# A chunked DeltaNet recurrence feeding a GELU network on one core: the factor g folded into the block inverse, one transposition replaced by ScalarE copies

## The chip, the core and the metric

The kernel runs on one core of a Trainium2 chip. The core has five engines, each with its own queue of instructions that it works through in order: TensorE (PE, matrix products; PEld is its loading of weights), VectorE (DVE), ScalarE (ACT), GpSimd (POOL) and SyncE (SP, which here only issues DMAs). The metric is the device time of one execution in microseconds (us), the median of several runs. The profile is of one execution, and its times count from that execution's start.

## What is computed

`B, H, S, D = 4, 8, 768, 48`. For each of the 32 pairs of batch and head a 48x48 state is carried over 768 steps; the outputs of all heads, laid side by side, are the input of a two-layer network with exact GELU.

```python
k_n = k / (norm(k) + 1e-6)
for t in range(S):
    y[:, :, t] = einsum('bhd,bhde->bhe', q[:, :, t], state)
    v_old      = einsum('bhde,bhd->bhe', state, k_n[:, :, t])
    state     += b_t * einsum('bhd,bhe->bhde', k_n[:, :, t], v_t - v_old)
x = y.transpose(0, 2, 1, 3).reshape(B * S, H * D)        # 3072 x 384
out = gelu(x @ w_in) @ w_out                              # 384 -> 2048 -> 384
```

The two weight matrices arrive as 64-bit floats and are turned into 32-bit ones on the chip. All arithmetic is in 32 bits.

## The kernel before

**Chunks and groups.** The 768 steps are cut into 12 chunks of 64. A tile holds one chunk of two batches: its 128 partitions are two halves `p` of 64 rows. There are two such tiles per chunk (`a` = 0, 1). Two chunks make a group `g` (six groups), with 32 units `u` (tile and head) for each half.

**The inverse of a group.** Inside a chunk the recurrence becomes a triangular system whose matrix is the Gram matrix of the keys, scaled row by row with `g = -beta/norm^2` (`gms`, made in `factors`, L263), plus the identity. Its inverse is built in 32x32 blocks. `eliminate_steps` (L422) does the diagonal blocks of all units at once on VectorE: `flip` (L432) transposes the blocks into `Nu` (L434) and multiplies by a mask that carries g (L435, made by GpSimd at L429), 30 calls of `eliminate` (L437) run two operations each (L442, L444), `diagonal` (L446) sets ones. `back` (L450) then transposes the result three times on VectorE: into `XM` (L453), into the right half of `Zf` (L457, columns 32 to 63), and into the left half of `Zf` (L457 again, columns 0 to 31). `clear` (L461) zeroes the lower rows of the left half, mostly by GpSimd memsets (L469).

**The joins.** The off-diagonal block is made of two small products per unit. Level 0 multiplies `XM` by the Gram block `G` into PSUM (`psJ`); VectorE multiplies this by g into the lower rows of `XM` (L498 in the first group, L528 in the others). Level 1 multiplies `Zf` by `XM`; ScalarE copies the result into the upper rows of the right half of `Zf` (L502, L532). `join` (L477) serves group 0, `join_run` (L504) the others, where the matmuls of level 0 of the later chunk and of level 1 of the earlier chunk are interleaved.

**The steps of a chunk.** `against_state` (L559) forms the products with the state (`psK`, L575), copies `y` (L582, ScalarE), subtracts V (L583, VectorE) and multiplies by g (L584, VectorE) to get W. In chunk 0, where the state is zero, GpSimd multiplies V by `ng` (L565; `ng` is made at L885). `solve` (L591) multiplies by `Zf` (`psU`, L600) and copies to U (L606, ScalarE). `use` and `update` form the output and the new state (L618, L627; `next_state` L632), `read` and `turn` bring x into `xT` (L639 or L641, L662, L663).

**The network.** `fc1` (L684) with the GELU on ScalarE (L686) fills G; `fc2` (L697, chunks 0 and 1) or seven half-size products (L722, later chunks) follow.

**The weights.** `begin`, `exponents`, `mantissas`, `signed` (L214 to L239) decode one of 16 parts: five VectorE operations (L218, L228, L230, L235, L236) with one ScalarE operation (L223) between L218 and L235. `fetch` (L199) loads the next part into the place that has come free.

**What sets the order.** Up to L916 all engines' orders are as written. Behind that a list of steps with due times, in chunks of the network (`plan`, L938), is sorted and issued; VectorE keeps this order, the other engines' orders are set by the scheduler that builds the program. Each engine then follows its own fixed order, and waits by semaphore. PSUM pool `dn` has two buffers and serves `psJ`, `psG`, `psK`, `psU` and `psY` in turn; `psH` and `psO` share two others.

Of the kernel before, what the change touches and what calls it, by code (L numbers as in the profile page):

```python
# [11 lines left out]
ALU = mybir.AluOpType  # L12
# [4 lines left out]
def kernel(  # L17
# [28 lines left out]
    nc = tc.nc  # L46
    B, H, S, D = q.shape
    DM, DF = moe_w_in.shape
    C = 64
# [371 lines left out]

    def eliminate_steps(g):  # L422
        steps = []

        def scales():
            gt = wk.tile([128, HB], F32, tag="gt", name="gt", bufs=1)
            gl = XMs[g] = wk.tile([128, NU, HB], F32, tag="XM", name="XM", bufs=1)
            nc.vector.transpose(gt, gms[g].rearrange("q t h -> q (t h)"))
            nc.gpsimd.tensor_tensor(gl, low, gt.unsqueeze(2).to_broadcast([128, HB, HB]),  # L429
                                    op=ALU.mult)  # L430

        def flip():  # L432
            Nus[g] = wk.tile([128, HB, HB], F32, tag="Nu", name="Nu", bufs=1)
            nc.vector.transpose(Nus[g], Ds[g].rearrange("q u n -> q n u"))  # L434
            nc.vector.tensor_tensor(Nus[g], Nus[g], XMs[g], op=ALU.mult)  # L435

        def eliminate(j):  # L437
            nu = Nus[g]
            n = HB - 1 - j
            tmp = wk.tile([128, HB * HB // 4], F32, tag="tmp", name="tmp")  # L440
            tmp = tmp[:, 0:n * j].rearrange("q (i c) -> q i c", i=n)
            nc.vector.tensor_tensor(tmp, nu[:, j + 1:, j:j + 1].to_broadcast([128, n, j]),  # L442
                                    nu[:, j:j + 1, 0:j].to_broadcast([128, n, j]), op=ALU.mult)
            nc.vector.tensor_tensor(nu[:, j + 1:, 0:j], nu[:, j + 1:, 0:j], tmp, op=ALU.add)  # L444

        def diagonal():  # L446
            flat = Nus[g].rearrange("q i c -> q (i c)")
            nc.vector.memset(flat[:, 0:HB * HB:HB + 1], 1.0)

        def back(x):  # L450
            nu = Nus[g]
            if x == 0:
                nc.vector.transpose(XMs[g].rearrange("q u c -> q c u"),  # L453
                                    nu.rearrange("q i c -> q c i"))
            else:
                cols = slice(HB, C) if x == 1 else slice(0, HB)
                nc.vector.transpose(Zf[g % 2][:, :, cols].rearrange("q u i -> q i u"), nu)  # L457
            if x == 2 and g > 0:
                clear(g)

        def clear(g):  # L461
                for cc in range(2):
                    for p in range(2):
                        part = Zf[g % 2][p * C + HB:(p + 1) * C,
                                         cc * NU // 2:(cc + 1) * NU // 2, 0:HB]
                        if g == cc == p == 0:
                            nc.scalar.mul(part, low[0:HB, 0:HB // 2], 0.0)
                        else:
                            nc.gpsimd.memset(part, 0.0)  # L469

        steps = [(0.3, scales), (3.0, flip)]
        steps += [(0.7, eliminate, j) for j in range(1, HB - 1)]
        steps += [(0.1, diagonal)]
        steps += [(1.9, back, x) for x in range(3)]
        return steps + [(0.0, clear, 0)] if g == 0 else steps

    def join(g, ts, level, copy=nc.scalar.copy):  # L477

        xm, zf, off = XMs[g], Zf[g % 2], Gs[g]
        gm = gms[g].rearrange("q t h -> q (t h)")  # L480
        psJ = dn("psJ").rearrange("q b (u n) -> q b u n", n=HB)
        for i, u in enumerate(range(ts[0] * H, (ts[-1] + 1) * H)):
            for p in range(2):
                top = slice(p * C, p * C + HB)
                low_ = slice(p * C + HB, (p + 1) * C)
                rows, to = (top, low_) if level == 0 else (low_, top)
                nc.tensor.matmul(psJ[to, i // (2 * H), i % (2 * H), :],
                                 lhsT=(xm if level else off)[rows, u, :],
                                 rhs=zf[rows, u, HB:C] if level else xm[rows, u, :],
                                 start=True, stop=True)  # L490
        for i in range(0, len(ts), 2):
            us = slice(ts[i] * H, (ts[min(i + 1, len(ts) - 1)] + 1) * H)
            n = us.stop - us.start
            for p in range(2):
                top = slice(p * C, p * C + HB)
                low_ = slice(p * C + HB, (p + 1) * C)
                if level == 0:
                    nc.vector.tensor_tensor(  # L498
                        xm[low_, us, :], psJ[low_, i // 2, 0:n],
                        gm[low_, us].unsqueeze(2).to_broadcast([HB, n, HB]), op=ALU.mult)  # L500
                else:
                    copy(zf[top, us, HB:C], psJ[top, i // 2, 0:n])  # L502

    def join_run(g, ts0, ts1):  # L504

        xm, zf, off = XMs[g], Zf[g % 2], Gs[g]
        gm = gms[g].rearrange("q t h -> q (t h)")
        sets = []
        for level, ts in enumerate((ts0, ts1)):
            if ts:  # L510
                psJ = dn("psJ")[:, 0].rearrange("q (u n) -> q u n", n=HB)
                sets.append((level, slice(ts[0] * H, (ts[-1] + 1) * H), psJ))
        for i in range(2 * H):
            for p in range(2):
                for level, us, psJ in sets:
                    u = us.start + i
                    top = slice(p * C, p * C + HB)
                    low_ = slice(p * C + HB, (p + 1) * C)
                    rows, to = (top, low_) if level == 0 else (low_, top)
                    nc.tensor.matmul(psJ[to, i, :], lhsT=(xm if level else off)[rows, u, :],  # L520
                                     rhs=zf[rows, u, HB:C] if level else xm[rows, u, :],
                                     start=True, stop=True)
        for level, us, psJ in sets:
            for p in range(2):
                top = slice(p * C, p * C + HB)
                low_ = slice(p * C + HB, (p + 1) * C)
                if level == 0:
                    nc.vector.tensor_tensor(  # L528
                        xm[low_, us, :], psJ[low_],
                        gm[low_, us].unsqueeze(2).to_broadcast([HB, 2 * H, HB]), op=ALU.mult)  # L530
                else:
                    nc.scalar.copy(zf[top, us, HB:C], psJ[top])  # L532

# [25 lines left out]
    def against_state(us):  # L559
# [17 lines left out]
        for u in us:  # L577
            if u.c == 0:
                continue
            gm = gms[u.c // 2][:, u.t]  # L580
            u.y = wk.tile([128, H, D], F32, tag="y", name="y")
            nc.scalar.copy(heads(u.y), u.psK[:, 1])  # L582
            nc.vector.tensor_tensor(heads(u.W), u.psK[:, 0], heads(u.V), op=ALU.subtract)  # L583
            nc.vector.tensor_tensor(u.W, u.W, gm.unsqueeze(2).to_broadcast([128, H, D]),  # L584
                                    op=ALU.mult)

    def quarters(ap):

# [261 lines left out]
    signs(0, 2)  # L850
    diagonals(first[3])
    root(n0)
    scales_, flip_, *rows, back0, back1, back2, clear_ = [s_[1:] for s_ in eliminate_steps(0)]
    factors(gms[0], beta_m[:, 0:2].rearrange("q c a h -> q (c a) h"), n0)
    scales_[0]()
    flip_[0]()
    ng = wk.tile([128, NA, H], F32, tag="ng", name="ng", bufs=1)
    for u in first:
        grams([u])
    signs(2, NC)  # L860
# [21 lines left out]
    grams(fourth)  # L882
    for fn, *args in rows:
        fn(*args)
    nc.vector.scalar_tensor_tensor(ng, gms[0][:, 0:NA], -1.0, ns[0], ALU.mult, ALU.mult)  # L885
    back0[0](*back0[1:])
    against_state(first[:NA])
    for u in first:
# [1 line left out]
    back1[0](*back1[1:])  # L890
    for a in range(NA):
        join(0, (a,), 0)
    back2[0](*back2[1:])
    for a in range(NA):
        join(0, (a,), 1)
    clear_[0](*clear_[1:])
    for u in first[NA:]:
        scale_v(u)
    begin(0)
# [27 lines left out]
    def late():  # L927
# [3 lines left out]
        for a in range(NA):  # L931
# [3 lines left out]
            for c in range(5, NC, 2):  # L935
# [4 lines left out]
    plan += [at(0.98, 0.985, [(1.0, load, 3)]),  # L940
             at(1.02, 1.1, [(1.0, join, 0, range(NA, 2 * NA), level) for level in range(2)]),
]
    sums = [(1.0, sum_of_squares, tiles[c, a], h) for c in (2, 3) for a in range(NA) for h in range(H)]
    plan += [at(1.08, 1.5, sums), at(1.51, 1.511, [(1.0, prep, c) for c in (2, 3)]), at(1.65, 1.655, [(1.0, finish_both)]), at(2.97, 2.971, [(1.0, finish, 4)]), at(2.725, 2.726, [(1.0, queries, third)]),
             at(1.12, 1.6, state_steps(1)),
             at(1.75, 2.45, eliminate_steps(1)),
             at(2.64, 2.77, join_steps(1)), at(2.76, 2.985, state_steps(2)),
             at(2.72, 2.721, [(1.0, prep, 4)]), at(2.8, 2.9, [(1.0, grams, [tiles[4, a] for a in range(NA)])])]
    plan += [at(0.995, 1.0, [(1.0, load_v, 2)]), at(2.98, 2.981, [(1.0, sums_of_w)]), at(3.1, 3.11, [(1.0, last_sum_of_w)])]
# [17 lines left out]
    for w in range(3, NC):  # L967
# [6 lines left out]
        if w % 2:  # L974
            plan += [at(w + 0.09, w + 0.092, gram + query), at(w + 0.25, w + 0.95, state_steps(w))]
            if two_ahead:
# [46 lines left out]
```

## Time and profile before

Median of three runs: 669.02 us (667.24, 669.02, 669.72). The profiled execution has a span of 667.6 us.

| engine | busy us | share of the span |
|---|---|---|
| PE | 643.4 | 96% |
| PEld | 563.6 | 84% |
| DVE | 451.9 | 68% |
| ACT | 228.5 | 34% |
| POOL | 82.3 | 12% |

Busy time by stage, from the view of windows (us from the start; DVE is VectorE):

| stage | PE | DVE | ACT | POOL | granted PE clock |
|---|---|---|---|---|---|
| 0 to 20 | 13.40 | 14.50 | 7.16 | 7.04 | 1.00 |
| 20 to 40 | 15.55 | 18.28 | 10.79 | 0.44 | 0.99 |
| 40 to 60 | 15.59 | 18.79 | 13.73 | 10.31 | 0.50 |
| 60 to 80 | 17.49 | 19.53 | 15.26 | 6.18 | 1.00 |
| 80 to 100 | 19.68 | 19.07 | 9.64 | 0.00 | 1.00 |
| 100 to 120 | 19.78 | 19.38 | 11.65 | 1.92 | 1.00 |
| 120 to 160 | 38.84 | 33.07 | 13.90 | 4.97 | 0.96 |
| 160 to 200 | 39.51 | 30.87 | 17.45 | 6.43 | 1.00 |
| 250 to 300 | 50.00 | 31.87 | 15.35 | 7.05 | 1.00 |

The durations that the operations of the change have in this profile, per instruction:

| operation | tile | mean us | count |
|---|---|---|---|
| L453, L457 transposition | 128x1024 | 2.07, 1.92 | 6, 12 |
| L435 VectorE multiply | 128x1024 | 1.23 | 6 |
| L528 VectorE multiply by g | 32x512 | 0.69 | 20 |
| L498 VectorE multiply by g | 32x256, 32x512 | 0.42, 0.69 | 4, 2 |
| L584 VectorE multiply by g | 128x384 | 0.56 | 22 |
| L469 GpSimd memset | 32x512 | 0.54 | 23 |
| L502 ScalarE copy from PSUM | 32x256, 32x512 | 0.36, 0.57 | 4, 2 |
| L532 ScalarE copy from PSUM | 32x512 | 0.57 | 20 |
| L385 ScalarE copy, SBUF to SBUF | 32x512 | 0.62 | 20 |

A busy share says little here: the stages have different limits. The chain of waits, followed back from the last instruction, tells which engine's work ended last at each point, and the timeline of one engine shows what it waited for (in brackets behind a row: how long it sat idle and which instruction released it). Matmul ends are modelled, and one 32-bit matmul has two records.

### The profile page before, as it was taken

The page shows a single profiled execution, that of the slowest core. Times are in us where ns is not written, and L with a number is a line of the kernel's source. Part 1 is how long each engine was busy: PE and PEld are TensorE (multiplying, and loading weights), DVE is VectorE, ACT ScalarE, POOL GpSimd, SP SyncE. Part 2 cuts the span into 40 slices and gives each one's busy share as a digit, 9 for nine tenths or more (in the row PEclk, how much of TensorE's full clock was granted, in tenths as well). Part 3 has the DMA queues.
Part 4 walks back from the last instruction along what each step waited for, and adds up shares of the span by engine and source line. Part 5 has one row for each costly group of instructions (what it writes and reads, how often), then busy time and mean ns, then how long its engine had stood idle before and what let it go on. Part 6 is the DMA issues. An engine that isn't in the chain of part 4 may idle for free.

```text
span 667.6 us, 21705 instructions
## 1 busy us (share of the span) xinstructions
PE 643.4 (96%) x9542; PEld 563.6 (84%) x9542; DVE 451.9 (68%) x921; ACT 228.5 (34%) x605; POOL 82.3 (12%) x82
## 2 busy tenths in 40 slices
PE   6877999999999999999999999999999999999997
PEld 5666776767789989989989989989989989989997
DVE  6999999994799845489846489846479844324022
ACT  3367755704432242242143142143142132122220
POOL 4050300103110021111021111021111010000000
PEclk9966999998999999999999999999999999999999
DMA  9885655303432232511332511211301210100101
GB/s 132 175 253 173 121 170 133 48 1 71 83 45 39 51 52 43 85 32 26 57 53 45 82 27 31 51 19 32 67 3 26 56 18 3 25 2 2 24 1 25
DMA packets 158431, 39.76 MB, mean 60 GB/s; under 512 B 150016, under 2 KB 153216, under 8 KB 158336
## 3 DMA queue, kind: packets, MB, share of 16 engines
q1 hardware_dynamic: 152464, 33.40, 26.5%
q10 hardware_dynamic: 5872, 4.97, 3.3%
q8 instruction: 75, 1.23, 0.8%
q14 instruction: 20, 0.16, 0.1%
HBM read 33.62 MB, written 4.72 MB: 57 GB/s over the span
## 4 chain that ended last, share of the span: by engine, by line
PE 86%; DVE 7%; ACT 3%; issue 2%; DMA 1%; SPq 0%; DVEq 0%
PE psH L684 36%; PE psX L722 12%; PE psY L722 12%; PE psO L697 5%; PE psZ L722 4%; PE psK L575 3%; PE psJ L520 3%; PE psG L367 3%; PE psU L600 2%; PE psY L618 2%; DVE Nu L444 2%; DVE tmp L442 2%; PE psY L627 1%; ACT U L606 1%; PE psX L662 1%
## 5 line engine op out<-in xcount | busy, mean ns | idle before, releaser
L684 PE MATMUL psH<-xT,w_in_sb 128*128 128x256 f32 x1152 | 261.4, 383 | 2.4 <-ACT G L686 2.3
L684 PEld LDWEIGHTS psH<-xT,w_in_sb 128*128 128x128 f32 x1152 | 215.7, 190 | 33.7 <-ACT G L686 3.5
L686 ACT ACTIVATE G<-psH 128x256 f32<-128x256 f32 x192 | 73.3, 382 | 181.8 <-PE psH L684 169.8
L444 DVE TENSOR_TENSOR Nu<-Nu,tmp 128x30 f32<-128x30 f32 (+9 forms) x180 | 62.9, 349 | 6.2
L442 DVE TENSOR_TENSOR tmp<-Nu 128x30 f32<-128x30 f32 (+9 forms) x180 | 60.5, 336 | 5.1
L722 PE MATMUL psX<-w_out_sb,G 128*128 128x192 f32 x320 | 56.2, 329 | 0.0
L722 PE MATMUL psY<-w_out_sb,G 128*128 128x192 f32 x304 | 54.1, 329 | 0.6
L722 PEld LDWEIGHTS psX<-w_out_sb,G 128*128 128x128 f32 x320 | 52.2, 190 | 0.7
L722 PEld LDWEIGHTS psY<-w_out_sb,G 128*128 128x128 f32 x304 | 49.1, 190 | 2.1 <-DVE u L768 1.8
L663 ACT COPY xT<-psX 128x384 f32<-128x384 f32 x24 | 11.4, 478 | 105.0 <-PE psX L662 105.0
L697 PE MATMUL psO<-w_out_sb,G 128*128 128x384 f32 x128 | 45.0, 498 | 0.0
L306 POOL TENSOR_TENSOR n<-n,half 128x16 f32<-128x16 f32 x10 | 29.4, 2937 | 88.2 <-DVE n L281 67.4
L402 DVE TENSOR_TENSOR P<-psG,mask 128x1024 f32<-128x1024 f32 x10 | 12.2, 1224 | 37.0 <-PE psG L367 37.0
L606 ACT COPY U<-psU 64x192 f32<-64x192 f32 x96 | 30.0, 313 | 21.0 <-PE psU L600 19.7
L697 PEld LDWEIGHTS psO<-w_out_sb,G 128*128 128x128 f32 x128 | 23.7, 191 | 14.4 <-DVE w_out_sb L236 0.6
L583 DVE TENSOR_TENSOR W<-psK,V 128x384 f32<-128x384 f32 x22 | 12.1, 552 | 28.8 <-ACT y L582 28.8
L469 POOL MEMSET Zf<- 32x512 f32 x23 | 12.4, 540 | 154.5 <-DVE Zf L457 153.6
L731 DVE TENSOR_TENSOR S<-G 128x512 f32<-128x512 f32 x20 | 13.7, 687 | 25.8 <-ACT G L686 25.7
L332 POOL TENSOR_TENSOR V<-V,n 128x384 f32<-128x384 f32 x18 | 17.3, 968 | 104.5 <-DMA V<-in_v_dram 69.2
L641 DVE TENSOR_TENSOR x<-psY,y 64x192 f32<-64x192 f32 x80 | 28.3, 354 | 0.9
L722 PE MATMUL psY<-T,G 128*128 128x192 f32 x160 | 28.2, 329 | 0.0
L722 PE MATMUL psX<-T,G 128*128 128x192 f32 x160 | 28.1, 329 | 0.0
(138 smaller groups left out, 871.4 us busy)
## 6 DMA issues: line engine op xcount, KB each, us to landing
Kp<-in_k_dram SPq DMA_DIRECT2D x76, 96.0 KB, 3.3
w_out_sb<-in_moe_w_in_dram SPq DMA_DIRECT2D x24, 256.0 KB, 4.3
V<-in_v_dram SPq DMA_DIRECT2D x48, 96.0 KB, 3.1
out_dram<-o_sb ACTq DMA_DIRECT2D x46, 96.0 KB, 2.2
w_raw<-in_moe_w_out_dram SPq DMA_DIRECT2D x10, 384.0 KB, 4.7
Zf<-in_moe_w_out_dram SPq DMA_DIRECT2D x6, 384.0 KB, 3.9
Qp<-in_q_dram SPq DMA_DIRECT2D x64, 32.0 KB, 2.1
Qp<-in_q_dram SPq DMA_DIRECT2D x16, 96.0 KB, 4.2
```

What stands on the lines that cost most here:

```text
L306: nc.gpsimd.tensor_tensor(flat, flat, half, op=ALU.pow)
L367: nc.tensor.matmul(psG[HALF[p], r, i * NP + j, :], lhsT=u.Kt[rows, p, j, :], rhs=(u.Qt if x else u.Kt)[rows, p, j, :], start=True, stop=True)
L442: nc.vector.tensor_tensor(tmp, nu[:, j + 1:, j:j + 1].to_broadcast([128, n, j]), nu[:, j:j + 1, 0:j].to_broadcast([128, n, j]), op=ALU.mult)
L444: nc.vector.tensor_tensor(nu[:, j + 1:, 0:j], nu[:, j + 1:, 0:j], tmp, op=ALU.add)
L520: nc.tensor.matmul(psJ[to, i, :], lhsT=(xm if level else off)[rows, u, :], rhs=zf[rows, u, HB:C] if level else xm[rows, u, :], start=True, ...
L575: nc.tensor.matmul(u.psK[to, x, r, j, :], lhsT=(u.Qt if x else u.Kt)[rows, p, j, :], rhs=St[rows, u.a, p, j, :], start=True, stop=True)
L606: copy(pairs(u.U[HALF[p]], s), u.psU[HALF[p ^ s], p])
L641: nc.vector.tensor_tensor(dst, src, pairs(u.y[HALF[p ^ s]], s), op=ALU.add)
L684: nc.tensor.matmul(psH, lhsT=w_in_sb[:, f // 2, m, f % 2 * 128:(f % 2 + 1) * 128], rhs=xTs[c][:, m, :], start=(m == 0), stop=(m == NM - 1))
L686: nc.scalar.activation(G[:, f, :], psH, ACT.Gelu)
L697: nc.tensor.matmul(u.psO, lhsT=G[:, f, u.a * 128:(u.a + 1) * 128], rhs=w_out_sb[:, f, :], start=(f == 0), stop=(f == NF - 1))
L722: nc.tensor.matmul(ps_, lhsT=lhs[:, f, :], rhs=rhs[:, f, :], start=first and f == 0, stop=f == FH - 1, skip_group_check=not first)
```

## The change

Once the inverse of the diagonal blocks is complete, its columns are multiplied by g (`weigh`, one VectorE operation of 128x1024 per group, between `diagonal` and the transpositions). The later products with g then fall away: the level-0 results are only copied (now by ScalarE), and W is only the difference. The third transposition of `back` is gone; in its place ScalarE copies the upper diagonal blocks from the right half of `Zf` to the left, in four copies of 32x512 per group (`top`: two for the earlier chunk's units, two for the later's), before level 1 overwrites the source. The zeros of the left half are written once per buffer of `Zf` (`clear`, two GpSimd memsets of 32x1024 each), not in every group. `ng` no longer needs g.

```diff
+        def weigh():
+            nc.vector.tensor_tensor(Nus[g], Nus[g],
+                                    gts[0].unsqueeze(1).to_broadcast([128, HB, HB]), op=ALU.mult)
         def back(x):
...
-                cols = slice(HB, C) if x == 1 else slice(0, HB)
-                nc.vector.transpose(Zf[g % 2][:, :, cols].rearrange("q u i -> q i u"), nu)
-            if x == 2 and g > 0:
-                clear(g)
+                nc.vector.transpose(Zf[g % 2][:, :, HB:C].rearrange("q u i -> q i u"), nu)
...
-        steps += [(1.9, back, x) for x in range(3)]
+        steps += [(0.1, diagonal), (1.2, weigh)]
+        steps += [(1.9, back, x) for x in range(2)]
+    def top(g, p, us):
+        part = Zf[g % 2][p * C:p * C + HB, us]
+        nc.scalar.copy(part[:, :, 0:HB], part[:, :, HB:C])
+    def clear(z):
+        for p in range(2):
+            nc.gpsimd.memset(z[p * C + HB:(p + 1) * C, :, 0:HB], 0.0)
...
-                    nc.vector.tensor_tensor(
-                        xm[low_, us, :], psJ[low_, i // 2, 0:n],
-                        gm[low_, us].unsqueeze(2).to_broadcast([HB, n, HB]), op=ALU.mult)
+                    copy(xm[low_, us, :], psJ[low_, i // 2, 0:n])
...
             nc.vector.tensor_tensor(heads(u.W), u.psK[:, 0], heads(u.V), op=ALU.subtract)
-            nc.vector.tensor_tensor(u.W, u.W, gm.unsqueeze(2).to_broadcast([128, H, D]),
-                                    op=ALU.mult)
...
     scales_[0]()
     flip_[0]()
+    clear(Zf[0])
...
-    nc.vector.scalar_tensor_tensor(ng, gms[0][:, 0:NA], -1.0, ns[0], ALU.mult, ALU.mult)
+    nc.vector.tensor_scalar_mul(ng, ns[0], -1.0)
...
     for a in range(NA):
         join(0, (a,), 0)
-    back2[0](*back2[1:])
+    for p in range(2):
+        top(0, p, EARLIER)
     for a in range(NA):
         join(0, (a,), 1)
-    clear_[0](*clear_[1:])
+    for p in range(2):
+        top(0, p, LATER)
...
+    plan += [at(1.7, 1.71, [(1.0, clear, Zf[1])]), at(0.98, 0.985, [(1.0, load, 3)]),
...
+             at(2.47, 2.6, top_steps(1, EARLIER) + top_steps(1, LATER)),
...
-                         at(w + 0.4, w + 1.06, rows[14:-3]), at(w + 1.07, w + 1.2, rows[-3:])]
+                         at(w + 0.4, w + 1.06, rows[14:-2]), at(w + 1.07, w + 1.16, rows[-2:]),
+                         at(w + 1.17, w + 1.29, top_steps(w // 2 + 1, EARLIER)),
+                         at(w + 1.305, w + 1.355, top_steps(w // 2 + 1, LATER))]
```

The level-0 copies of `join_run` (the other groups) are changed in the same way as those of `join`. In the changed program as built, TensorE's order stays as it was but for three places of the second layer of chunk 0 (where two matmuls change sides with a transposition or a join), and ScalarE's queue takes in the copies. For group 1 it holds, one behind the other: the last eight GELUs of chunk 1's first layer, four `top` copies, two squares of k (L278), two level-0 copies of the earlier chunk, two of the later one, then the level-1 copies. In the later groups three `top` copies stand in front of the sixth GELU of the chunk then under way, and one behind it.

More of the change, by code (lines that the diff above doesn't have):

```diff
@@ L423, in eliminate_steps @@
         steps = []
+        gts = []
         def scales():
             gt = wk.tile([128, HB], F32, tag="gt", name="gt", bufs=1)
+            gts.append(gt)
             gl = XMs[g] = wk.tile([128, NU, HB], F32, tag="XM", name="XM", bufs=1)
@@ L455, in back, with top_steps @@
             else:
-                cols = slice(HB, C) if x == 1 else slice(0, HB)
-                nc.vector.transpose(Zf[g % 2][:, :, cols].rearrange("q u i -> q i u"), nu)
-            if x == 2 and g > 0:
-                clear(g)
[L461 to L469, printed above, removed]
+                nc.vector.transpose(Zf[g % 2][:, :, HB:C].rearrange("q u i -> q i u"), nu)
         steps = [(0.3, scales), (3.0, flip)]
         steps += [(0.7, eliminate, j) for j in range(1, HB - 1)]
-        steps += [(0.1, diagonal)]
-        steps += [(1.9, back, x) for x in range(3)]
-        return steps + [(0.0, clear, 0)] if g == 0 else steps
+        steps += [(0.1, diagonal), (1.2, weigh)]
+        steps += [(1.9, back, x) for x in range(2)]
+        return steps
+    def top(g, p, us):
+        part = Zf[g % 2][p * C:p * C + HB, us]
+        nc.scalar.copy(part[:, :, 0:HB], part[:, :, HB:C])
+    EARLIER, LATER = slice(0, NA * H), slice(NA * H, NU)
+    def top_steps(g, us):
+        return [(1.0, top, g, p, us) for p in range(2)]
+    def clear(z):
+        for p in range(2):
+            nc.gpsimd.memset(z[p * C + HB:(p + 1) * C, :, 0:HB], 0.0)
     def join(g, ts, level, copy=nc.scalar.copy):
         xm, zf, off = XMs[g], Zf[g % 2], Gs[g]
-        gm = gms[g].rearrange("q t h -> q (t h)")
         psJ = dn("psJ").rearrange("q b (u n) -> q b u n", n=HB)
@@ L506, in join_run @@
         xm, zf, off = XMs[g], Zf[g % 2], Gs[g]
-        gm = gms[g].rearrange("q t h -> q (t h)")
         sets = []
@@ L527, in join_run @@
                 if level == 0:
-                    nc.vector.tensor_tensor(
-                        xm[low_, us, :], psJ[low_],
-                        gm[low_, us].unsqueeze(2).to_broadcast([HB, 2 * H, HB]), op=ALU.mult)
+                    nc.scalar.copy(xm[low_, us, :], psJ[low_])
                 else:
@@ L579, in against_state @@
                 continue
-            gm = gms[u.c // 2][:, u.t]
             u.y = wk.tile([128, H, D], F32, tag="y", name="y")
@@ L852 @@
     root(n0)
-    scales_, flip_, *rows, back0, back1, back2, clear_ = [s_[1:] for s_ in eliminate_steps(0)]
+    scales_, flip_, *rows, back0, back1 = [s_[1:] for s_ in eliminate_steps(0)]
     factors(gms[0], beta_m[:, 0:2].rearrange("q c a h -> q (c a) h"), n0)
@@ L939 @@
     plan += [at(0.985, 1.26, decode_steps(3, n_in)), at(1.26, 1.65, decode_steps(n_in, NW)), at(1.66, 1.67, [(1.0, late)])]
-    plan += [at(0.98, 0.985, [(1.0, load, 3)]),
+    plan += [at(1.7, 1.71, [(1.0, clear, Zf[1])]), at(0.98, 0.985, [(1.0, load, 3)]),
              at(1.02, 1.1, [(1.0, join, 0, range(NA, 2 * NA), level) for level in range(2)]),
```

## The prediction

> **What bounds the kernel now.** I read the engine shares first, then the chain of waits, then the timelines around the only places where TensorE stands still. TensorE is busy for 643.4 of 667.6 us. From 200 us on it is idle for about 0.1 us in 50, so nothing that VectorE or GpSimd saves there can shorten the run. Its idle time lies before 72 us and at one later place, which the chain of waits shows:
>
> ```profile
> 145.72 2.14 PE psJ L520 x128
> 147.87 1.49 PE psO L697 x4
> 149.35 1.17 issue
> 150.52 1.20 PE psJ L520 x63
> ```
>
> Columns: start, us, what. These are group 1's joins: both chunks' level 0, two matmuls of the second layer, 1.17 us of nothing, then the earlier chunk's level 1. VectorE's timeline (start, us, engine, line, operation) tells why:
>
> ```profile
> 143.32 2.11 DVE L453 STREAM_TRANSPOSE XM<-Nu 128x1024 f32<-128x1024 f32 x1
> 145.32 3.68 DVE L457 STREAM_TRANSPOSE Zf<-Nu 128x1024 f32<-128x1024 f32 x2
> 149.03 2.82 DVE L528 TENSOR_TENSOR XM<-psJ,gm 32x512 f32<-32x512 f32 x4
> ```
>
> Level 1 needs the first two L528, which end at 149.03+1.41 = 150.44; TensorE starts at 150.52. VectorE has been busy since 88 us (decoding, then row steps) with one gap of 0.2 us, so **VectorE's own sequence sets the moment at which TensorE's unbroken stretch to the end can begin**. The gap costs twice. The windows of half a microsecond (window, length, PE, PEld, DVE, ACT, POOL, granted clock, DMA) show the clock halved after it:
>
> ```profile
> 151.50:152.00 0.50, 0.50 (x14) 0.41 (x9) 0.47 (x2) 0.00 (x0) 0.00 (x0) 1.00 0.00 0
> 152.50:153.00 0.50, 0.50 (x2) 0.32 (x1) 0.39 (x1) 0.50 (x2) 0.00 (x0) 0.50 0.00 0
> 155.00:155.50 0.50, 0.50 (x32) 0.50 (x28) 0.00 (x0) 0.09 (x1) 0.50 (x1) 0.50 0.22 24
> 156.00:156.50 0.50, 0.50 (x44) 0.50 (x38) 0.50 (x1) 0.00 (x0) 0.00 (x0) 1.00 0.60 96
> ```
>
> One more wait decides how much VectorE can gain ahead of this. It is the only one of VectorE's between 60 and 119 us:
>
> ```profile
> 83.64 2.58 ACT L606 COPY U<-psU 64x192 f32<-64x192 f32 x8 [0.72 <-PE psU L600]
> 86.25 0.66 ACT L686 ACTIVATE G<-psH 128x256 f32<-128x256 f32 x2
> 86.80 0.94 ACT L223 ACTIVATE w_e<-w_e,lim 128x768 uint32<-128x768 uint32 x1
> ...
> 87.76 0.96 DVE L235 SCALAR_TENSOR_TENSOR w_e<-Zf,w_e 128x768 uint32<-128x768 uint32 x1 [0.58 <-ACT w_e L223]
> ```
>
> The decode waits for L223, which stands in ScalarE's queue behind the copies of U, which wait for TensorE.
>
> [...] half clock from about 152.2 to 155.7[...]. [...] L228 takes 0.97 and 1.19 us beside GpSimd at 47 to 51 us, 0.55 elsewhere.
>
> **The change, part by part.**
>
> *Start, to 59 us.* After the row steps (39.4) VectorE gets `weigh`. No such row exists; the same size with a full second input is L435, 1.23; between 1.15 and 1.3 (a repeated input could read cheaper or not). So `XM` is ready at 42.85 instead of 41.57 and `Zf`'s right half at 44.8 instead of 43.4. GpSimd's W and P (L565, L405) move by the same 1.3 and are not late: P was done at 46.1 and is read at 51. VectorE drops four L498 (1.75) and the second L457 (1.93), so it reaches the decode at 44.7 instead of 47.0. ScalarE's queue grows. From TensorE's first level-0 half (44.1): two copies of 0.36, wait for the second half (45.2), two more to 46.0, two `top` at L385's 0.62 to 47.2, four level-1 copies (L502, 1.45) to 48.7, two `top` to 49.95, L223 to 50.9, then U. Before, U began at 50.59: +0.3. From there to 59 us the chain runs U, L223, x, xT, L223 on ScalarE, so VectorE's 2.3 us end as waiting, whatever GpSimd's products beside the decode (44.7 to 49.6) cost it. The first set of GpSimd memsets moves to about 16 us, where GpSimd had nothing until 39 us.
>
> *59 to 88 us.* VectorE drops two L498 (1.41) and two L584 (1.06): it would be 2.47-0.3, about 2.1 us ahead. ScalarE takes two copies of 0.57 between GELUs; counting its queue from 62.8 us (L223 0.83, squares 0.23, GELU 0.27, as they follow each other in the trace) the GELU that TensorE waits for at 72.25 comes within 0.5 us of before, rather earlier. TensorE's `psU` then ends 0 to 0.5 earlier than its 83.6, and U, one GELU (two before) and L223 let L235 start at about 87.0 instead of 87.76. VectorE waits there for over a microsecond: **of 2.1 us, 0.8 remain**, 0.3 to 1.3.
>
> *88 to 143 us.* Same instructions. The second `clear` (two memsets of about 1 us at some 112 us) lies beside decode operations of L228's kind: 0 to 1 us, I take 0.4. The row steps end 0.4 us earlier than 143.2.
>
> *Group 1's joins.* VectorE: 143.32-0.4 = 142.9, `weigh` to 144.15, `XM` to 146.2, right half to 148.15. ScalarE: four `top` 2.47, two L278 as they follow each other 0.95, two level-0 copies 1.15, waits 0.15 together: 4.7 us behind the transposition, in a queue that had been idle for 14 us before. Level 1 starts at **152.85 instead of 150.52: +2.3**. TensorE, there by 149.3, can't step over it. What is queued behind: the rest of the second layer, `psG`, the later level 1. From level 1's start to the end of the later level 1 the old trace has 150.52 to 157.0, 6.5 us, of which 3.4 at half clock: 4.8 at full clock, and one second-layer matmul (0.65) is now behind: 5.45. With the half clock until 155.7, 1.4 is done by then and 4.05 is left: 159.75, +2.7. If [...] half speed lasts to 159.1: 161.5, +4.4. [...] I take the middle, **+3.5**.
>
> *Groups 2 to 5.* VectorE loses 2.76 (L528), 2.2 (L584), 1.92 and gains 1.23 for each, all beside a full TensorE: 0. Three `top` copies now precede a GELU. In the old trace TensorE needs this GELU's buffer at 236.7 in group 2; VectorE reaches its end of transposition at about 233.9 (L779 at 225.4, row steps 0.4, `weigh`, four short transpositions 2.5, two long ones 3.9), three copies to 235.75, GELU done by 236.15. Slack 0.5: 0, up to 1 us a group. The level-0 copies (0.57 for 0.69, ending about 238.6) are needed at 239.5: 0. The memsets that fall away waited on nobody's path (0.3 us once). DMAs are neither added nor moved; SP's queue is passed by nothing.
>
> Sum on the profile's span: 667.6+3.5 = 671.1. The runs' median is 1.4 above that span, so **672.5**, 0.52% slower. A measurement of this kernel can tell about 0.5%, 3.3 us, from no change.
>
> **The rivals.**
> 1. *Not slower: VectorE keeps its 2.1 us.* If `psU` comes over a microsecond earlier (ScalarE's queue at 62 to 72 us would have to speed up that much), the wait at L235 vanishes. Level 1 then starts at 151.1, the old half-clock window is the only one, and the later level 1 ends at 158.2: +1.2, 670.2. It decides from a lead of some 1.5 us. For it: VectorE's 2.5 us are real. Against: 2.6 us of U copies stand before L223 in both programs.
> 2. *Worse: the `top` copies hold GELUs in groups 2 to 5.* If VectorE is over 0.5 us later there than I count (GpSimd's V products have stretched row steps from 0.41 to 0.99), TensorE stands still for 0.5 to 1 us in each of four groups on top of the 3.5: 676. For it: no other slack is so small. Against: memsets and four L528 have left.
> 3. *Faster.* U starts earlier than before (copies at 0.4 rather than 0.62)[...]: level 1 at 150.3, no window lost: some 665.5. Against: 152.85 would have to fall by 2.5 us.
>
> **How the numbers follow.** Forecast 0.57 (from 671.7 with one half-clock window to 673.4 with two, about half on each side of 672.4), rival 1 0.26, rival 2 0.12, rival 3 0.05. Faster by over 0.5%: 0.05. Within: 0.26 and 0.24 of the forecast, 0.50. Slower: 0.33 and 0.12, 0.45. The forecast's own range is 671.2 to 674; leaving out rival 3 and the upper part of rival 2, the range is 669.0 to 676.0.
>
> **What would show it.** Right: idle of about 3.5 us on TensorE before group 1's first level 1, released by a ScalarE copy into `XM`; four `top` copies directly behind VectorE's transposition; a halved clock for 3.4 to 7 us behind it; a wait of a microsecond or more at L235's counterpart near 87 us; U near 50.9. Wrong: level 1 before 151 us, VectorE without a wait near 87 us, or idle TensorE of over 0.5 us near each later join.

## The result and the profile after

The changed kernel takes 674.78 us (median of four runs, 674.23 to 676.54); the kernel before, run beside it, 668.47 us. The ratio is **1.0102, 95% interval 1.0083 to 1.0122**: 1% slower. The profiled executions have spans of 672.9 and 667.6 us, a difference of 5.3 us. All that follows is accounted on spans. The other microsecond of the medians is not in it: every execution takes 1.7 to 1.9 us more than its span, so the changed kernel's profile is of a typical execution, but the old kernel's is of one that was 0.9 us slower than its median.

The chain of waits at group 1's joins (start, us, what), where the old kernel had 1.17 us of nothing:

```profile
148.59 0.05 ACT Zf L474
...
150.50 0.61 ACT Zf L474
151.12 0.03 issue
151.14 0.94 ACT ksq L278 x2
152.10 0.58 ACT XM L533
152.69 0.59 ACT XM L533
153.28 0.04 issue
153.32 1.42 PE psJ L525 x64
154.74 3.51 PE psO L697 x6
158.25 1.09 PE psG L367 x64
159.34 1.13 PE psJ L525 x64
```

TensorE stands still for 3.28 us until 153.32, and every step in front of it is on ScalarE: four `top` copies (L474), two squares (L278), the first two level-0 copies (L533). VectorE's timeline ahead of that, in the same columns as before:

```profile
143.42 1.23 DVE L454 TENSOR_TENSOR Nu<-Nu,gt 128x1024 f32<-128x1024 f32 x1
144.68 2.06 DVE L460 STREAM_TRANSPOSE XM<-Nu 128x1024 f32<-128x1024 f32 x1
146.65 1.92 DVE L463 STREAM_TRANSPOSE Zf<-Nu 128x1024 f32<-128x1024 f32 x1
148.42 0.94 DVE L281 TENSOR_REDUCE n<-ksq 128x8 f32<-128x384 f32 x2
```

The new multiplication (L454) costs 1.23 us, as the operation of its size did before; VectorE is through at 148.57, 0.5 us before the first L528 began in the old kernel, and then has only a reduction to do. The windows of half a microsecond show the clock (the last three figures are granted clock, DMA share, GB/s):

```profile
152.50:153.00 0.50, 0.00 (x0) 0.00 (x0) 0.00 (x0) 0.49 (x2) 0.00 (x0) 1.00 0.00 0
154.50:155.00 0.50, 0.50 (x11) 0.44 (x7) 0.00 (x0) 0.16 (x1) 0.00 (x0) 0.50 0.93 181
156.50:157.00 0.50, 0.50 (x2) 0.24 (x1) 0.00 (x0) 0.00 (x0) 0.00 (x0) 0.50 0.00 0
157.50:158.00 0.50, 0.50 (x3) 0.14 (x1) 0.00 (x0) 0.00 (x0) 0.00 (x0) 1.00 0.06 6
```

Half clock from about 154.1 to 157.5 (by windows of a quarter of a microsecond): 3.4 us of it again, begun later. The later level 1 ends at 160.48 instead of 157.00: **+3.5 us**.

The rest is at a second place, 380 us later. ScalarE's timeline, then TensorE's, at group 5's joins (in brackets the idle time before, and who ended it):

```profile
537.12 0.38 ACT L686 ACTIVATE G<-psH 128x256 f32<-128x256 f32 x1 [0.91 <-PE psH L684]
538.99 1.90 ACT L474 COPY Zf<-Zf 32x512 f32<-32x512 f32 x3 [1.49 <-DVE Zf L463]
540.80 0.37 ACT L686 ACTIVATE G<-psH 128x256 f32<-128x256 f32 x1
```

```profile
531.74 7.93 PE L684 MATMUL psH<-xT,w_in_sb 128*128 128x256 f32 x36
541.22 1.56 PE L684 MATMUL psH<-xT,w_in_sb 128*128 128x256 f32 x6 [1.54 <-ACT G L686]
```

A GELU stands behind three `top` copies, which wait for VectorE's transposition; TensorE waits 1.54 us for the GELU. In the old kernel these are 42 unbroken matmul records:

```profile
528.26 9.23 PE L684 MATMUL psH<-xT,w_in_sb 128*128 128x256 f32 x42
```

**The account.** Behind the start TensorE has hardly any other idle time (0.1 us in 50), so the distance between two landmarks on it measures what a stretch lost. I use the starts of level 0 in groups 1, 2 and 5 (from TensorE's timeline), in us:

| kernel | span | level 0, group 1 | to group 2 | group 2 to 5 |
|---|---|---|---|---|
| before | 667.6 | 145.65 | 88.75 | 303.01 |
| changed | 672.9 | 146.99 | 90.89 | 304.83 |
| ... with group 1's top copies on VectorE | 674.1 | 146.81 | 92.19 | 304.96 |
| ... with group 5's top copies on VectorE | 671.3 | 146.84 | 91.29 | 303.02 |
| fold alone | 670.8 | 147.25 | 90.39 | 303.01 |
| third transposition alone | 673.0 | 146.02 | 87.84 | 308.64 |
| changed, group 1's level-0 copies on VectorE | 667.5 | 146.54 | 85.94 | 304.80 |
| the same, and group 5's top copies on VectorE | 666.7 | 147.57 | 85.94 | 303.02 |
| third alone, top copies of groups 2 to 5 on VectorE | 664.0 | 144.86 | 85.94 | 303.01 |

Where nothing waits the middle stretch is 85.94 and the last 303.01; the old kernel, too, lost 2.8 us in the middle one, and the changed one 5.0 there and 1.8 in the last. In both, the loss in the middle is the idle time, 1.17 and 3.28 us, and about 1.7 us more, half of the 3.4 us at half clock. The difference between the two is 2.1 + 1.8 us, and 1.3 us by which level 0 of group 1 starts later; the later level 1, which waits for the copies in any case, is 3.5 us later for the first and the third together. The first column contains the start, which differs by up to a microsecond between executions of one program: the copies of U begin at 50.67 to 51.69 in seven programs that are alike up to there. What makes this difference is not shown.

### The profile page after: what moved, and what is told of

Read it like the earlier page. It is cut to its first block, busy times and chain, and to the rows that moved or that the text cites. A ratio compares the mean times of both kernels' runs of the same rounds, so it can differ in the third digit from the quotient of the medians.

```text
span 672.9 us, 21675 instructions
## 1 busy us (share of the span) xinstructions
PE 643.0 (96%) x9542; PEld 562.7 (84%) x9542; DVE 419.9 (62%) x873; ACT 256.4 (38%) x654; POOL 75.8 (11%) x63
## 3 DMA queue, kind: packets, MB, share of 16 engines
q8 instruction: 75, 1.23, 0.8%
## 4 chain that ended last, share of the span: by engine, by line
PE 77%; DVE 14%; ACT 5%; issue 2%; DMA 1%; POOL 1%; SPq 0%; DVEq 0%; ACTq 0%; POOLq 0%
PE psH L684 32%; PE psX L722 12%; PE psY L722 12%; PE psZ L722 4%; PE psK L578 3%; DVE Nu L446 3%; DVE tmp L444 3%; PE psJ L525 3%; PE psG L367 3%; PE psU L600 2%; PE psO L697 2%; PE psY L618 2%; DVE w_e L235 1%; PE psY L627 1%; DVE w_out_sb L236 1%
## 5 line engine op out<-in xcount | busy, mean ns | idle before, releaser
L722 PE MATMUL psZ<-T,S 128*128 128x192 f32 x160 | 27.6, 326 | 0.0
```

Source lines behind the costliest of these rows:

```text
L722: nc.tensor.matmul(ps_, lhsT=lhs[:, f, :], rhs=rhs[:, f, :], start=first and f == 0, stop=f == FH - 1, skip_group_check=not first)
```

## The experiments

Each run is timed against the kernel before on the same chip; ratios are to it. The first four share one theory A: ScalarE's top copies in front of other work are the delay at both places. Against it stands B, VectorE's longer chain, in the first three, and C, that top copies cost wherever they stand, in the fourth.

**1. Group 1's top copies on VectorE.**

```diff
     def top(g, p, us):
-        nc.scalar.copy(part[:, :, 0:HB], part[:, :, HB:C])
+        copy = nc.vector.tensor_copy if g in (1,) else nc.scalar.copy
+        copy(part[:, :, 0:HB], part[:, :, HB:C])
```

> Group 1's four top copies go from ScalarE to VectorE, which has nothing else then; all else as in the changed kernel. Theory A (ScalarE's queue: 2.5 us of top copies and 0.95 us of squares stand between the transposition at 148.57 and the level-0 copies): the first two level-0 copies run at about 148.3 to 149.4, both level 0 and the second layer's products fill TensorE to 150.6, level 1 starts at 150.6 instead of 153.3, the later level 1 ends at about 156 without a half clock, 157.6 with one (160.48 in the changed kernel): 3 to 4.5 us off the span, 668.4 to 670. Theory B (VectorE's chain is what got too long: weigh's 1.2 us and the lost lead): level 1 still after 152 us, at most 1 us off the span, about 672.

674.98 us, ratio 1.0108 (1.0094 to 1.0122), span 674.1: not better than the changed kernel. Theory A as stated falls, and B's forecast, level 1 after 152 us, came true. But VectorE's and then ScalarE's timeline show another cause than the length of VectorE's chain:

```profile
148.42 1.71 DVE L475 COPY Zf<-Zf 32x512 f32<-32x512 f32 x4
150.14 1.01 DVE L281 TENSOR_REDUCE n<-ksq 128x8 f32<-128x384 f32 x2
```

```profile
150.72 0.98 ACT L278 ACTIVATE ksq<-Kp 128x384 f32<-128x384 f32 x2 [11.16 <-DVE n L281]
151.73 2.35 ACT L534 COPY XM<-psJ 32x512 f32<-32x512 f32 x4
```

ScalarE now waits 11 us with nothing to do. The squares of a later chunk's keys (L278) stand ahead of the level-0 copies in its queue, and they wait until VectorE's reduction (L281) has emptied one of their two buffers; VectorE comes to that behind its top copies. In the changed kernel the reduction ran beside ScalarE's top copies, so this wait could not be seen. Level 1 starts at 152.95, and the later one ends at 161.60, for here the clock is at half for 6.8 us (153.0 to 159.8).

**2. Group 5's top copies on VectorE** (the same edit with `g in (5,)`).

> Only group 5's four top copies go from ScalarE to VectorE. Theory A: the GELU that TensorE waits for at 541.2 no longer stands behind three copies, TensorE's 1.54 us of idle time and the 0.28 us after it vanish: 1.8 us off the span, about 671.1, and nothing changes at group 1 (level 1 at 153.3). Theory B (VectorE is late there, with its weigh and the transpositions of Q in front): level 0 is held by XM or by the second transposition in place of the GELU, under 0.5 us off the span, about 672.7.

673.38 us, ratio 1.0083 (1.0069 to 1.0097), span 671.3. The wait at group 5 is gone (303.02), group 1 is nearly as in the changed kernel (level 1 at 153.13, but 1.92 us long in place of 1.42, as in experiment 1, where it runs at half clock; the middle stretch is 0.4 longer). A holds here, and group 5's price of 1.8 us is shown; the two ratios' intervals overlap, so it rests on the trace.

**3. The fold alone.**

The diff is to the changed kernel; the memsets come back with the third transposition.

```diff
-        steps += [(1.9, back, x) for x in range(2)]
+        steps += [(1.9, back, x) for x in range(3)]
...
-    for p in range(2):
-        top(0, p, EARLIER)
+    back2[0](*back2[1:])
...
-             at(2.47, 2.6, top_steps(1, EARLIER) + top_steps(1, LATER)),
```

> The g folding alone: VectorE's third transposition and the memsets of each group are back, no top copies on any engine. TensorE's order is that of the changed kernel. Theory A: level 1 of group 1 at about 150.6, the later level 1 ends at 156 to 157.6, no idle TensorE at group 5, U of chunk 0 about 0.5 us earlier (some 50.6): span 666 to 668, so about as before or up to 0.3% faster than it. Theory B (weigh's 1.2 us on VectorE's chain is the cause, a third transposition in front of nothing changes little): as slow as the changed kernel within 1 us, 672.

672.64 us, ratio 1.0071 (1.0059 to 1.0084), span 670.8: neither theory's number. Group 5 has no wait, as A said. At group 1 the squares wait once more for the reduction, this time behind the third transposition, and level 1 starts at 153.12. ScalarE's timeline:

```profile
150.90 0.97 ACT L278 ACTIVATE ksq<-Kp 128x384 f32<-128x384 f32 x2 [10.90 <-DVE n L281]
```

So no top copy is needed for the delay; it is enough that the level-0 copies have moved to ScalarE, behind the squares.

**4. The third transposition alone** (from the kernel before: `back` with two transpositions, `top`, `top_steps` and `clear` as in the change; no `weigh`).

> The other half alone, built from the kernel before: the third transposition becomes four top copies on ScalarE per group, zeros written once; no weigh, VectorE still multiplies the level-0 results and W by g. TensorE's order is that of the kernel before. Theory A: the level-0 products with g run on VectorE right behind the second transposition (147.3), beside the top copies, so level 1 starts at about 149.4, where TensorE arrives, instead of 150.5; the later level 1 ends 1 to 2.4 us earlier than before's 157.0; at group 5 the GELU is held by about 0.4 us: span 665.5 to 667.5, not slower than before. Theory C (the top copies are the costly part wherever they stand): slower than before by 2 us or more, 670 and above.

674.40 us, ratio 1.0095 (1.0080 to 1.0111), span 673.0: far from A's 665.5 to 667.5, and by the number what C said. Yet group 1 behaved as A said: VectorE does the level-0 products itself at 147.65, level 1 starts at 149.72 where TensorE arrives, no half clock (1.00 granted from 148 to 155), the later one ends at 154.56 (157.00 before). But all of groups 2 to 5 lost. TensorE's timeline has three of the waits:

```profile
232.36 1.56 PE L686 MATMUL psH<-xT,w_in_sb 128*128 128x256 f32 x6 [1.63 <-ACT G L688]
335.05 1.56 PE L686 MATMUL psH<-xT,w_in_sb 128*128 128x256 f32 x6 [1.41 <-ACT G L688]
437.73 1.56 PE L686 MATMUL psH<-xT,w_in_sb 128*128 128x256 f32 x6 [1.41 <-ACT G L688]
```

and ScalarE's timeline shows how, at the second:

```profile
331.08 0.39 ACT L688 ACTIVATE G<-psH 128x256 f32<-128x256 f32 x1 [0.91 <-PE psH L686]
333.35 1.24 ACT L467 COPY Zf<-Zf 32x512 f32<-32x512 f32 x2 [1.88 <-DVE Zf L456]
334.61 0.38 ACT L688 ACTIVATE G<-psH 128x256 f32<-128x256 f32 x1
```

Here the scheduler has put the top copies ahead of the *fifth* GELU of the chunk. In the changed kernel they stand ahead of the sixth in groups 2 to 4, and ahead of the fifth in group 5 alone. GELUs follow each other at 1.29 us, so one place in the queue is worth about the wait. No experiment moved the copies by one place; that the place matters is read from groups 2 to 4 of the changed kernel, where the same copies stand one GELU later and TensorE waits for nothing.

Out of these four came a theory A2: **what delays group 1 is whatever stands in front of the level-0 copies in ScalarE's queue, the squares included; what delays the later groups is the place of the top copies among the GELUs.**

**5. Group 1's level-0 copies on VectorE**, top copies and squares left on ScalarE.

```diff
                 if level == 0:
-                    nc.scalar.copy(xm[low_, us, :], psJ[low_])
+                    copy = nc.vector.tensor_copy if g in (1,) else nc.scalar.copy
+                    copy(xm[low_, us, :], psJ[low_])
```

> Group 1's level-0 copies go to VectorE, directly behind its second transposition; the top copies and the squares stay on ScalarE. Theory A2 (ScalarE's queue in front of the level-0 copies is the delay: top copies and, in their absence, the squares, which wait for VectorE's reductions): the first two copies are done by 149.9, level 1 starts at about 150.6, where TensorE arrives, with no half clock as in the run of the third transposition alone (4.84 us from there to the end of the later level 1): 155.5 instead of 160.48, span 668, i.e. 672.9 - 5.0. Theory B (VectorE's chain with weigh is too long for any engine to make it good): level 1 after 152, span over 671.

669.76 us, ratio 1.0028 (1.0017 to 1.0038), span 667.5, against 668 expected. The chain of waits is unbroken TensorE work:

```profile
146.61 2.14 PE psJ L525 x128
148.75 1.49 PE psO L698 x4
150.24 1.13 PE psJ L525 x64
151.37 1.49 PE psO L698 x4
152.86 1.09 PE psG L367 x64
153.95 1.13 PE psJ L525 x64
```

`weigh` is still there, and VectorE's transposition ends at 148.13, only 0.4 us earlier than in the changed kernel (the start was that much earlier); B falls. This one edit takes back 5 us of the loss. What it leaves is group 5 (304.80).

**6. and 7. The squares behind the joins**, once with group 1's top copies on VectorE, once with them on ScalarE.

```diff
-             at(2.72, 2.721, [(1.0, prep, 4)])
+             at(2.80, 2.801, [(1.0, prep, 4)])
```

> As the first experiment (group 1's top copies on VectorE), but with the reductions of chunk 4's squares later in VectorE's order, so that chunk 5's squares, which wait for them, stand behind the joins in ScalarE's queue. ScalarE has nothing in front of the level-0 copies then. Theory A2: copies at about 148.4, level 1 at 150.6, later level 1 ends at 155.5: span about 668, 6 below the first experiment. Theory B: no change against the first experiment, 674.

> The changed kernel with only the squares moved behind the joins as in the run before; the four top copies stay in front of the level-0 copies on ScalarE. Theory A2: level 1 earlier by the 0.95 us of the squares, 152.35 instead of 153.3, still a gap of 1.8 us and a halved clock: span 671 to 672. It is the dose between the changed kernel (3.5 us in front of the copies) and the run before (0). Theory B: no change, 673.

In both, chunk 4's squares are taken of chunk 5's keys, since the load of these stands ahead of the step in the order as written; number and size of the operations stay. So both compute something else than the reference, and count for their times alone.

The first: 671.79 us, ratio 1.0066 (1.0047 to 1.0085), span 673.7; the profile is of the slowest of six executions, whose spans go from 668.6 to 673.7. At group 1 it does what A2 says: level-0 copies at 148.16, level 1 at 149.92, the later one ends at 155.41. But the span is not 668, for TensorE has a new wait of 2.97 us at 176.49, in front of a transposition of x; ScalarE's timeline:

```profile
175.55 0.52 ACT L278 ACTIVATE ksq<-Kp 128x384 f32<-128x384 f32 x1 [6.41 <-DMA Kp<-in_k_dram]
175.98 0.46 ACT L664 COPY xT<-psX 128x384 f32<-128x384 f32 x1
```

The moved squares now wait for a load, with the copy of x behind them: the same mechanism at another place. From that transposition to the next one of Q's tiles TensorE then takes 7.89 us (5.10 in the changed kernel), at a halved clock from 175.9 to 182.7. Together that is 5.8 us, the difference between 668 and the span. Half of the six executions lost less than 2 us against 668; how much of the new wait they have is not shown.

The second: 675.60 us, ratio 1.0111 (1.0097 to 1.0126), span 674.5. Level 1 starts at 152.39 (152.35 expected), 0.93 earlier than in the changed kernel: the dose of two squares. Yet its later level 1 ends at 160.99, 0.5 later. The windows show the clock at half from 152.3 to 159.1, 6.8 us in place of 3.4 (and TensorE waits 0.90 us at 180.01 behind the moved squares, as in the first):

```profile
153.00:154.00 1.00, 1.00 (x46) 1.00 (x42) 0.00 (x0) 0.53 (x1) 0.00 (x0) 0.50 0.00 0
158.00:159.00 1.00, 1.00 (x25) 0.63 (x28) 0.00 (x0) 0.48 (x1) 0.00 (x0) 0.50 0.00 0
```

**8. The third transposition alone, the top copies of groups 2 to 5 on VectorE** (experiment 4 with the edit of experiment 1 for `g in (2, 3, 4, 5)`).

> The third transposition alone (no fold), with the top copies of groups 2 to 5 on VectorE, group 1's on ScalarE. In the run of this part alone TensorE stood still for 1.4 to 1.6 us before a GELU in each of groups 2 to 5, because the top copies stand in front of the fifth GELU there, while group 1 was 2.4 us better than in the kernel before. Theory A2: these four waits vanish, group 1 stays (later level 1 ends at 154.6): 673.0 less 4 times 1.9 = 665.3, about 0.3% faster than before. Theory C (top copies cost wherever they are): still above 669.

665.89 us, ratio **0.9970 (0.9959 to 0.9981)**, span 664.0: faster than both kernels. The four waits are gone (303.01), group 1 is at its least (85.94). Of the 3.6 us on the spans 2.8 are group 1's joins, 0.8 the start. By the medians the gain is 2.0 us: 667.6 is a high span for the old kernel, whose 49 executions beside experiments 9 to 11 have a median span of 666.1. A copy of 32x512 that takes ScalarE 0.62 us takes VectorE 0.42.

**9. The whole change with both places mended** (experiments 5 and 2 together).

> The whole change with both places mended: group 1's level-0 copies and group 5's top copies on VectorE, all else as in the changed kernel. If the two waits are all that made the change slower, the savings add: 667.5 of the run with group 1 mended less the 1.8 us of group 5: 665.7, about 0.15 to 0.3% under the kernel before by its span, within 0.2% of it by the runs. If something else is left in groups 2 to 5 or in the start, it stays above 667.

668.03 us, ratio 0.9994 (0.9981 to 1.0007), span 666.7. Both stretches are without a wait (85.94 and 303.02): the two savings add, and nothing is left in groups 2 to 5. The span is 1.0 over the expectation because level 0 of group 1 starts 1.03 later than in experiment 5; U began 1.02 later in this execution. So the change, mended, is worth nothing that can be measured. On the profiles its joins gain 2.8 us and its first 147 us lose 1.9; by the medians, as the old kernel's profile is of a slow execution, nothing is left of the difference. A part of what keeps it behind experiment 8 is seen in its order: TensorE waits 0.94 us at 101 us for VectorE to decode weights (L236). Eight profiles with the fold show this wait (0.93 or 0.94 us), the four without the fold don't (the order of TensorE's second-layer matmuls is another there); in the changed kernel TensorE waits for group 1's joins in any case, so it cost nothing there. The rest of what the first 147 us lose is not located.

**10. and 11. Group 0's later top copies behind the transposition of x**, in experiment 9's kernel and in experiment 8's.

```diff
-    for p in range(2):
-        top(0, p, LATER)
...
     for u in first[:NA]:
         turn(u)
+    for p in range(2):
+        top(0, p, LATER)
```

> As the run before, and in group 0 the later chunk's two top copies come behind the transposition of x in place of in front of L223 and U (1.25 us of ScalarE's queue less there). If they hold U (50.7 to 51.1 in the changed kernel's start, 50.6 before), U starts up to 0.5 us earlier and so does everything to group 1's joins: 665.2 to 665.5. If TensorE's psU holds it, no change: 665.7.

> The third transposition alone with groups 2 to 5's top copies on VectorE (the fastest so far, 664.0 by its span), and group 0's later top copies behind the transposition of x. If they hold U, 0.3 to 0.5 us faster, 663.6; if not, 664.0 to 665, since the start of this program differs from run to run by up to 1 us.

669.21 us, ratio 1.0016 (1.0009 to 1.0023), and 667.11 us, ratio 0.9989 (0.9982 to 0.9996): each about 0.2% slower than the kernel it was made from, which neither expectation foretold. ScalarE's timeline of the first:

```profile
50.69 2.64 ACT L608 COPY U<-psU 64x192 f32<-64x192 f32 x8 [1.48 <-PE psU L602]
...
58.14 1.25 ACT L475 COPY Zf<-Zf 32x512 f32<-32x512 f32 x2
59.42 0.94 ACT L223 ACTIVATE w_e<-w_e,lim 128x768 uint32<-128x768 uint32 x1
```

U waits 1.48 us for TensorE: the copies in front of it had filled that wait. Behind it they lie on the chain U, L223, x, xT, L223: from U to this L223 it takes 8.73 us here, 7.45 in experiment 9.

## Why the prediction was right and where it was wrong

Foretold were 672.5 us and "slower", with the joins of group 1 as cause; measured were 674.8, inside the range of 669.0 to 676.0 and above the forecast's own, 671.2 to 674. By the spans +3.5 was foretold and +5.3 came: the joins are two thirds of it, and the rest is a step that was put at nothing. The signs named for a right forecast are all there.

*Start.* `weigh` 1.23, `XM` 43.08 (42.85 foretold), right half 44.89 (44.8), VectorE at the decode 44.75 (44.7), U 51.08 (50.9). Right; the 0.2 lies within what U's start differs by between executions. Rival 3 did not come: U began 0.5 us later than before, and the half clock that ended at 60.1 in the old kernel ended at 61.9.

*59 to 88 us.* Wrong in size: **of VectorE's 2.1 us nothing remained, not 0.8**. L235's counterpart starts at 87.82 with a wait of 1.57 us (87.76 and 0.58 before):

```profile
87.82 0.96 DVE L235 SCALAR_TENSOR_TENSOR w_e<-Zf,w_e 128x768 uint32<-128x768 uint32 x1 [1.57 <-ACT w_e L223]
```

This is one execution; in experiments 2, 5 and 9, alike up to there, it starts at 87.38 to 88.41. The argument, L223 behind U behind TensorE, was right. But I let TensorE arrive at `psU` up to 0.5 us earlier, and it came 0.33 later: its wait for the GELU at 72.58 grew from 0.50 to 0.72 us, and U began at 83.97. Rival 1 (the lead is kept) is refuted by the same line.

*88 to 143 us.* The second `clear` was to cost 0.4, an estimate of mine from the two long L228 of the start (0.97 and 1.19 us in place of 0.55); the L228 that lies beside these memsets (113.39) takes 0.56. From L235's start to the first operation behind the row steps it is 55.60 us (55.56 before), so it cost nothing that can be seen. The prediction counted the same instructions here, and did not see that TensorE's new order makes it wait 0.93 us for L236 at 101.21; nor does it mention two small waits of the old TensorE behind 72 us (0.32 at 86.69, 0.22 at 102.96).

*Group 1's joins.* Mechanism, engine and order right: +3.5 foretold and +3.5 measured. Level 1 at 153.32 in place of 152.85, the missing lead; then 3.4 us of half clock. The prediction took the middle between two sums, +2.7 with a half clock of that length and +4.4 with twice it; the second was my estimate, and nothing at the joins of the old kernel shows one so long. Two errors nearly cancelled: the 0.5 us by which level 1 came later, and the 0.8 us between the middle and the first sum. That +3.5 met +3.5 is in part luck. And the sum "4 top, 2 L278, 2 copies" treated the squares as 0.95 us of work. They are also a wait for VectorE's reduction; the top copies hid it, and a forecast for a version without them, which I did make for experiment 1, missed by 4 to 6 us.

*Groups 2 to 5.* This step failed: **"Slack 0.5: 0, up to 1 us a group"**. It is right for groups 2 to 4, which lost nothing: the copies ahead of the sixth GELU end where TensorE still has level 0 and the Gram products to do. It was worked out for group 2 alone and carried over. Group 5 makes no Gram products for a next chunk, its top copies stand one GELU earlier, and it lost 1.54 us of waiting and 0.28 around it. The text of the change says "the sixth GELU" of all later groups; for group 5 that is not so. Rival 2 had the mechanism, and wrong the place and the reason: one group by 1.8, not four by 0.5 to 1, and not because VectorE is late (in group 5 its second transposition ends 2.2 us before level 0 would have begun without the wait, in group 2 only 0.8).

The sum: +3.5 and +1.8 give the 5.3 us. The prediction set the old kernel's median 1.4 us above its profiled span; the changed kernel's lies 1.9 above its own.

Two readings carried the prediction through, and the runs show both. ScalarE took up its queue in order: in experiment 1 copies whose input was there at about 149 waited until 151.73 behind two squares. And TensorE's clock was at half for 3.4 us behind the gap, in the old kernel (152.2 to 155.7) and in the changed one (154.1 to 157.5); in experiments 1 and 7 it was 6.8 us. For experiment 3 I estimate 3.4 us from its durations: level 1 takes 1.62 us in place of 1.13 at full clock, the six matmul records behind it 3.28 in place of 2.09 (2.78 for eight), so 1.7 us are lost at half speed. The idle times before level 1 were 1.17, 3.28 and 2.81 us where half clock lasted 3.4, and 3.08 and 2.29 where it lasted 6.8, so its length can't be foretold from the idle time; what sets it is not shown. Idle times of 1.41 to 1.63 us in experiment 4 were followed by no half clock at all (1.00 granted from 160 to 650 us). There TensorE had 128x128 products on both sides, at group 1's joins 32x32 ones too; that this makes the difference is not shown.

## What to carry to other kernels

When an operation is given to another engine, read that engine's queue at the place where it lands and follow each instruction ahead of it to what *it* waits for: here two small squares hung on a reduction on the very engine that was to be relieved, and to take 2.5 us of copies away from in front of them brought the start of level 1 forward by only 0.4 us. A slack belongs to one pass of a loop; work it out again for the last pass, where the fillers of the others are missing. And a change of two parts is to be tried as its parts: either alone was also slower here, each for a reason of its own. One line took away the third transposition's (experiment 8) and turned it into a gain of 0.3%; for the fold such a line was tried only within the whole change (experiments 5 and 9).

## What the runs showed that was not expected

Where nothing waits, the landmarks' distances repeat to 0.01 us: 85.94 in three programs of the table and 303.01 or 303.02 in five, while the first 147 us differ by up to a microsecond between executions. A wait of 0.2 us can therefore be priced in one profile, where it lies behind the start. The half clocks that the windows show between 150 and 185 us lasted 3.4 us (the old kernel and the changed one) or 6.8 (experiments 1, 6 and 7). Idle TensorE of 2.3 to 3.3 us cost up to 3 us more by the clock: from level 1's start to the later one's end it takes 4.84 us at full clock (experiments 4 and 5), 7.16 with 3.4 us of half clock (the changed kernel) and 8.6 with 6.8 (experiments 1 and 7), with four matmul records of the second layer between them in the first case and six in the other two. The loss in the middle stretch can be estimated from the trace as the idle time and half of the half-clock time behind it: 2.9, 5.0, 4.5 and 6.5 us in the old kernel, the changed one and experiments 3 and 1, where the landmarks give 2.8, 5.0, 4.5 and 6.3.
